# Products of the identity with itself ahead of eleven early TensorE operations

## The chip, the cores and the metric

The kernel runs on one core of a Trainium2 chip. The core has a matrix engine (TensorE, in the profile PE for its matmuls and PEld for its weight loads), a vector engine (VectorE, DVE), a scalar engine (ScalarE, ACT), GpSimd (POOL) and the engine whose queue issues the transfers (SyncE, SP). Each takes its own instructions in the order in which they stand; they wait for each other on semaphores. The metric is the device time of one execution in microseconds, as the median of the runs.

## The reference

Two attentions follow each other (32 packed queries `p` attend to `k` and `v`; then `q` attends to the packed result), and the output goes through two feed-forward blocks:

```python
p_packed = sm_attn(p, k, v)                 # batch 8, heads 8, seq 576, head_dim 64
out = sm_attn(q, p_packed, p_packed)
x = out.transpose(0, 2, 1, 3).reshape(B * S, H * D)          # 4608 x 512
h = x @ w_in                                # d_ff 1024
solu = h * softmax(h)
ln = (solu - mu) / np.sqrt(var + 1e-06) * g_ln
y = ln @ w_out
r = np.maximum(y @ w2_in, 0.0)              # d_ff 2048
return (r * r) @ w2_out
```

The weights arrive as 64-bit floats and are turned into 32-bit ones on the chip.

## The kernel before

All work is first put into a list: `plan.op` and `plan.either` note an operation with its engine, a function that issues its instructions, and the buffers that it reads and writes. There are 5182 such operations, numbered as they are noted. `Plan.emit` (lines 372 to 396) then goes through the table `ORDER` (line 22), written out by hand, and issues the operations in that order. Since each engine takes its instructions in order, `ORDER` is each engine's queue.

For each of the 8 batches, `pack` (the first attention) issues on TensorE: the scores `s1` of `p` and `k` (`scores`, matmul in line 661), three groups of three transposes `pt` of the exponentials (line 725), the products `ppp` with `v` (line 736), and three transposes `ptp` (lines 752 and 753). `unpack` (the second attention) issues the scores `s2` of `q` (line 661 again) and the products `pg` of the packed result with `w_in` (line 672, `tiles8`), which become the tile `G`. `h_tile` issues the products `ph` of the attention weights with `G` (line 832 for the first batch, in plain 32-bit floats; line 855 for later ones and for the tile that spans two batches) and the transposes `ptv` of the normalised result (line 899). `y_stage` multiplies by `w_out` (lines 555 to 557). The second feed-forward block follows from about 463 us.

Between those TensorE operations VectorE and ScalarE do the softmax (maxima `mx`, line 691; exponentials `e`, line 708; copies `eT` of the transposes, line 537; scalings `pp` and `pd`, lines 740 and 742; transposes `a` of the second scores, line 770; sums `d`, line 795) and, in the same queues, the decoding of the weights (lines 570 to 601).

The results of all these products except `ph` lie in four PSUM banks that are shared. A bank is bound to a buffer when the first operation that names the buffer is issued, and goes back to the end of a list of free banks after the last one that does:

```python
    def bank(name):
        return psm.tile([P, 512], F32, name, tag="m", bufs=4, shared=True)
...
                    if b in uses and b.slot is None:
                        b.slot = free.setdefault(b.ring, list(range(b.ring.bufs))).pop(0)
```

`s1` and `s2` take all four banks at once; the `ph` tiles have two places of two banks each in another pool. The first matmul into a buffer waits until the engines that read the bank's buffer before have done so. A plain 32-bit product issues two weight loads and two matmuls on the chip, a transpose one of each: the 72 products of `ppp` in the code are 144 matmuls in the profile, the 9 transposes of `pt` are 9.

## Time and profile before

| | us |
|---|---|
| median of 3 runs | 1197.12 |
| lowest and highest | 1196.34, 1198.63 |
| the profiled execution | 1201.08 |
| its span, from the first to the last instruction | 1199.3 |

| engine | busy us | share of the span |
|---|---|---|
| TensorE matmuls | 1153.4 | 96% |
| TensorE weight loads | 1079.8 | 90% |
| VectorE | 918.8 | 77% |
| ScalarE | 757.5 | 63% |
| GpSimd | 128.9 | 11% |

The shares are means over the whole span, and the change is about its first 80 us. [...] The clock is listed as a mean over a stretch, from events that are recorded from 42.9 us on.

### The profile page before, as it was taken

The numbers are of one execution on the slowest core, as the hardware profiler recorded it, in microseconds if no ns is written. First come the engines' busy times: TensorE is split into PE (matmuls) and PEld (weight loads), VectorE is DVE, ScalarE is ACT, GpSimd is POOL, SyncE is SP. The second block draws the span as 40 slices with busy tenths as digits, with TensorE's granted clock in tenths as the row PEclk, the third lists the DMA queues.
The fourth block names the chain that finished last, engine by engine and source line by source line (L and its number), as shares of the span: only waits on it lengthen the run. The fifth ranks groups of instructions, "written<-read, shape, count | busy, mean of one in ns | idle before, by whom it ended". The sixth has DMA issues, their size and how long they took to land.

```text
span 1199.3 us, 26114 instructions
## 1 busy us (share of the span) xinstructions
PE 1153.4 (96%) x10044; PEld 1079.8 (90%) x10044; DVE 918.8 (77%) x1849; ACT 757.5 (63%) x1600; POOL 128.9 (11%) x137
## 2 busy tenths in 40 slices
PE   2689999999999999999999999999999999999998
PEld 1347988878898999999999999999999999999998
DVE  6999897898868853778878676734888888888885
ACT  7687766767677673576745667876545454545452
POOL 1344233023222310000000000000000000000000
PEclk9899999999999999999999999999999999999999
DMA  9633564445225499878674648557983626262602
GB/s 332 232 110 111 165 188 155 149 134 154 64 88 161 141 283 329 286 222 255 212 235 165 231 157 261 175 184 255 406 304 92 191 74 189 76 190 75 192 19 54
DMA packets 171080, 218.80 MB, mean 182 GB/s; under 512 B 17353, under 2 KB 133577, under 8 KB 170185
## 3 DMA queue, kind: packets, MB, share of 16 engines
q1 hardware_dynamic: 170089, 216.32, 55.5%
q8 instruction: 79, 1.29, 0.4%
q10 hardware_dynamic: 864, 0.79, 0.3%
q14 instruction: 48, 0.39, 0.1%
HBM read 131.08 MB, written 85.98 MB: 181 GB/s over the span
## 4 chain that ended last, share of the span: by engine, by line
PE 87%; DVE 5%; DMA 3%; ACT 3%; issue 1%; SPq 1%; POOL 0%; DVEq 0%; ACTq 0%
PE px L555 10%; PE px L557 10%; PE px L556 10%; PE ph L855 8%; PE py L555 5%; PE py L557 5%; PE py L556 5%; PE pa L555 5%; PE pa L557 5%; PE pa L556 5%; PE pz L555 3%; PE ptv L899 2%; PE pz L556 2%; PE pz L557 2%; PE s L661 2%; PE pg L672 1%
## 5 line engine op out<-in xcount | busy, mean ns | idle before, releaser
L537 ACT CAST cb<-ga 128x384 fp32r<-128x384 f32 x336 | 168.0, 514 | 163.2 <-PE pa L557 70.1
L540 DVE TENSOR_TENSOR cb<-ga,cb 128x384 fp32r<-128x384 f32 x336 | 180.4, 553 | 59.2 <-ACT cb L537 57.8
L555 PE MATMUL py<-v,wo 128*128 128x256 f32 x576 | 167.0, 290 | 0.9 <-ACT ysb L922 0.6
L557 PE MATMUL py<-v,wo 128*128 128x256 f32 x576 | 162.8, 283 | 0.0
L556 PE MATMUL py<-v,wo 128*128 128x256 f32 x576 | 162.7, 282 | 0.0
L557 PE MATMUL px<-oi,cb 128*128 128x256 f32 x504 | 142.2, 282 | 0.8 <-DVE cb L540 0.8
L555 PE MATMUL px<-oi,cb 128*128 128x256 f32 x504 | 142.2, 282 | 0.6 <-ACT gw L1135 0.6
L556 PE MATMUL px<-oi,cb 128*128 128x256 f32 x504 | 142.0, 282 | 0.0
L555 PE MATMUL pa<-oi,cb 128*128 128x256 f32 x504 | 142.0, 282 | 0.0
L557 PE MATMUL pa<-oi,cb 128*128 128x256 f32 x504 | 142.0, 282 | 0.0
L556 PE MATMUL pa<-oi,cb 128*128 128x256 f32 x504 | 142.0, 282 | 0.0
L555 PE MATMUL px<-y,zi 128*128 128x384 f32 x384 | 130.1, 339 | 1.7 <-ACT gw L1104 1.5
L557 PE MATMUL px<-y,zi 128*128 128x384 f32 x384 | 129.6, 337 | 0.0
L556 PE MATMUL px<-y,zi 128*128 128x384 f32 x384 | 129.5, 337 | 0.0
L555 PEld LDWEIGHTS py<-v,wo 128*128 128x128 f32 x576 | 110.0, 191 | 5.2 <-issue 2.1
L556 PEld LDWEIGHTS py<-v,wo 128*128 128x128 f32 x576 | 110.2, 191 | 0.9
L557 PEld LDWEIGHTS py<-v,wo 128*128 128x128 f32 x576 | 110.0, 191 | 0.0
L1048 DVE TENSOR_TENSOR ga<-ga 128x384 f32<-128x384 f32 x192 | 100.3, 551 | 5.1 <-DMA ga<-g_dram 4.2
L1104 ACT COPY gw<-px 128x384 f32<-128x384 f32 x144 | 67.2, 477 | 55.8 <-PE px L557 39.7
L1108 DVE TENSOR_TENSOR gw<-pz,gw 128x384 f32<-128x384 f32 x96 | 52.9, 553 | 62.0 <-PE pz L557 37.8
L557 PEld LDWEIGHTS px<-oi,cb 128*128 128x128 f32 x504 | 95.4, 189 | 1.1 <-DVE cb L540 1.1
L555 PEld LDWEIGHTS px<-oi,cb 128*128 128x128 f32 x504 | 95.4, 189 | 0.8 <-ACT gw L1135 0.8
(144 smaller groups left out, 2874.3 us busy)
## 6 DMA issues: line engine op xcount, KB each, us to landing
g_dram<-gw SPq DMA_DIRECT2D x192, 192.0 KB
ga<-g_dram SPq DMA_DIRECT2D x96, 384.0 KB
zi<-z_dram SPq DMA_DIRECT2D x28, 512.0 KB
oi<-o_dram SPq DMA_DIRECT2D x24, 512.0 KB
kr<-in_k_dram SPq DMA_DIRECT2D x16, 576.0 KB
vr<-in_v_dram SPq DMA_DIRECT2D x16, 576.0 KB
qr<-in_q_dram SPq DMA_DIRECT2D x16, 576.0 KB
y_dram<-ysb SPq DMA_DIRECT2D x72, 128.0 KB
```

The lines of the kernel that those rows point to most:

```text
L537: plan.op(ACT, c_act(cols, sbuf=r[0].pool not in (psm, psh, pso)), at, lambda: nc.scalar.copy(out_(), in_()), r=r, w=w)
L540: plan.either(on(cols, *engines), at, lambda e: vec[e].tensor_tensor(out_(), in_(), hi_().bitcast(F32), op=ALU.subtract), r=r, w=w, port=i ...
L555: nc.tensor.matmul(ps, lh, rh, start=first, stop=False, skip_group_check=onto)
L556: nc.tensor.matmul(ps, lh, rl, start=False, stop=False, skip_group_check=onto)
L557: nc.tensor.matmul(ps, ll, rh, start=False, stop=last, skip_group_check=onto)
L661: nc.tensor.matmul(banks[g][u]()[32 * e:32 * e + 32, :SH].rearrange("p (m t) -> p m t", t=T), lhs(ps, e, f), ts[e // 2]()[ps, e % 2, :, f] ...
L672: nc.tensor.matmul(banks[g]()[32 * e:32 * e + 32, :n], lhs()[ps, 32 * e:32 * e + 32], rhs(ps, g, e), start=True, stop=True)
L855: nc.tensor.matmul(ph()[:, fs], al[l]()[:, g], g_tiles[b, g]()[:, r, fs], start=ends[0] and g == 0 and t == 0, stop=ends[1] and g == NG - ...
L899: nc.tensor.transpose(pt()[:, c * P:(c + 1) * P], e()[:, (4 * t + c) * P:(4 * t + c + 1) * P], ident)
L1048: plan.op(DVE, c_dve(cols), at, lambda: nc.vector.tensor_tensor(out_(), in0(), in1(), op=op), r=r, w=w, port=True)
L1104: plan.op(ACT, c_act(HN), when(p, SN), lambda: nc.scalar.copy(t(), ps()[:, :HN]), r=[ps], w=[t])
L1108: plan.op(DVE, c_dve(HN), when(p, SN), lambda: nc.vector.tensor_tensor(t(), ps()[:, :HN], t(), op=ALU.add), r=[t, ps], w=[t])
```

## The change

Ahead of eleven TensorE operations, `emit` now issues a number of products of the 128 x 128 identity `ident` (plain 32-bit) with itself. They are written into the first 128 columns of the first PSUM buffer of the operation that follows, which begins that buffer anew with its own first product. Nothing reads what they leave.

```diff
+WARM = {9: 44, 30: 20, 36: 9, 41: 9, 77: 1, 82: 1, 161: 4, 196: 15, 182: 1, 207: 2, 375: 3}
...
-    def emit(self):
+    def emit(self, warm):
...
+                if i in WARM:
+                    warm(next(b for b in o.bufs if b.pool and b.pool.kw.get("space") == PSUM), WARM[i])
                 o.fn(list(o.engines)[i in second])
...
     second()
-    plan.emit()
+
+    def warm(b, n):
+        for _ in range(n):
+            nc.tensor.matmul(b()[:, :P], ident, ident, start=True, stop=True, skip_group_check=True)
+
+    plan.emit(warm)
```

The keys are numbers of operations. In the order of TensorE's queue, with the place in the profile of before:

| operation | what it is | starts at us | products ahead of it |
|---|---|---|---|
| 9 | `s1`, batch 0 | 15.62 | 44 |
| 30 | first three of the nine `pt`, batch 0 | 23.33 | 20 |
| 36 | `ppp`, batch 0 | 27.93 | 9 |
| 41 | `ptp`, batch 0 | 32.71 | 9 |
| 77 | `s2`, batch 0 | 34.07 | 1 |
| 82 | first half of `pg`, batch 0 | 38.61 | 1 |
| 161 | `s1`, batch 1 | 43.87 | 4 |
| 196 | first half of the first `ph` tile | 49.45 | 15 |
| 182 | first `pt`, batch 1 | 53.78 | 1 |
| 207 | first `ptv` | 68.74 | 2 |
| 375 | fifth `ph` tile | 76.70 | 3 |

That is 109 products, or 218 matmuls and 218 weight loads.

## Rows read from the trace of the kernel before

**Rows 1.** The page's busy tenths in 40 slices of the span, TensorE.
```profile
PE   2689999999999999999999999999999999999998
```

**Rows 2.** Waits of VectorE, 13 to 77 us: total, times, longest.
```profile
DVE a L770 <- PE s L661: 1.0, 1, 1.0
DVE d L795 <- ACT a L793: 0.8, 1, 0.8
```

**Rows 3.** Timeline of TensorE's matmuls: start, us, operation, count [idle before, releaser].
```profile
15.62 2.59 PE L661 MATMUL s<-kT,pT 32*32 32x288 f32 x64 [15.62 <-DVE pT L683]
23.33 2.15 PE L725 MATMUL pt<-ident,e 128*128 128x128 f32 x9 [5.13 <-ACT e L708]
27.93 2.27 PE L736 MATMUL ppp<-vr,eT 64*32 64x64 f32 x144 [2.44 <-ACT eT L537]
32.71 0.69 PE L752 MATMUL ptp<-ident,pd 128*128 128x128 f32 x2 [2.52 <-DVE pd L742]
...
34.07 1.17 PE L661 MATMUL s<-qT,ppf 32*32 32x288 f32 x2 [0.46 <-ACT ppf L537]
35.51 2.62 PE L661 MATMUL s<-qT,ppf 32*32 32x288 f32 x62 [0.27 <-issue]
38.61 3.91 PE L672 MATMUL pg<-wi,ppq 64*32 64x512 f32 x32 [0.48 <-DVE a L770]
43.87 1.59 PE L661 MATMUL s<-kT,pT 32*32 32x288 f32 x64 [1.34 <-ACT G L537]
49.45 3.78 PE L832 MATMUL ph<-G,aT 128*128 128x512 f32 x4 [3.99 <-DVE aT L802]
53.78 1.20 PE L725 MATMUL pt<-ident,e 128*128 128x128 f32 x9 [0.55 <-ACT e L708]
...
58.48 1.66 PE L736 MATMUL ppp<-vr,eT 64*32 64x64 f32 x144
...
68.74 1.06 PE L899 MATMUL ptv<-ident,e 128*128 128x128 f32 x8 [0.76 <-ACT ph L874]
69.64 3.60 PE L832 MATMUL ph<-G,aT 128*128 128x512 f32 x8
...
76.70 5.40 PE L855 MATMUL ph<-G,ah 128*128 128x512 f32 x8 [0.97 <-ACT ph L874]
...
102.17 2.30 PE L672 MATMUL pg<-wi,ppq 64*32 64x512 f32 x32
```

**Rows 4.** The page's costliest groups, weight loads of the `py` products: busy, mean ns | idle before.
```profile
L555 PEld LDWEIGHTS py<-v,wo 128*128 128x128 f32 x576 | 110.0, 191 | 5.2 <-issue 2.1
```

**Rows 5.** TensorE by stretches: length, busy (matmuls), mean granted clock, DMA share, GB/s.
```profile
40.00:42.00 2.00, 2.00 (x24) 1.00 0.00 0
...
46.00:48.00 2.00, 0.00 (x0) 0.58 1.02 385
...
52.00:54.00 2.00, 1.45 (x4) 0.71 1.02 354
...
76.00:78.00 2.00, 1.30 (x2) 0.76 0.94 312
```

**Rows 6.** Timeline of the other engines, 1 to 45 us.
```profile
1.15 0.29 POOL masks.py:199 TENSOR_SCALAR_AFFINE_SELECT ident<-ident 128x128 f32<-128x128 f32 x1
...
21.20 0.50 ACT L708 ACTIVATE e<-s,nmx 128x288 f32<-128x288 f32 x1 [1.62 <-DVE nmx L704]
...
26.97 1.28 ACT L537 COPY eT<-pt 128x384 f32<-128x384 f32 x3
...
31.71 0.43 DVE L740 TENSOR_SCALAR pp<-ppp,rs 128x64 f32<-128x64 f32 x2
...
35.71 1.22 DVE L586 SCALAR_TENSOR_TENSOR wraw<-wraw 128x1024 f32<-128x1024 uint32 x1
...
37.98 1.57 DVE L770 STREAM_TRANSPOSE a<-s 128x288 f32<-128x288 f32 x4 [1.05 <-PE s L661]
...
44.48 1.41 DVE L795 TENSOR_REDUCE d<-a 128x18 f32<-128x576 f32 x2 [0.76 <-ACT a L793]
```

## The prediction

> **What bounds the kernel now.** The page's slices come first [rows 1]: from the fourth slice on TensorE is busy nine tenths or more, and each slice is 30 us. The end is therefore the moment at which TensorE begins to be fed without a break, plus a sum of matmuls that the change leaves as it is. Only what moves the first 80 us moves the end.

> Which engine sets the pace in those 80 us is read from VectorE's waits [rows 2]. In 64 us it waits for TensorE's stage twice, 1.05 us ahead of `a` and 0.76 us ahead of `d` [rows 6]. Apart from those two places its queue goes on whatever TensorE does, so an earlier TensorE can give the early stretch at most 1.05 + 0.76 = 1.81 us. TensorE's own timeline [rows 3] then shows gaps of 0.3 to 5.1 us and the same operation at two paces: `s1` 2.59 us at 15.62 and 1.59 us at 43.87, `pt` 2.15 and 1.20, `pg` 3.91 and 2.30, four `ph` matmuls 3.78 us where eight take 3.60.

> The clock by stretches [rows 5] explains the later slow places. A mean of 0.58 over 46 to 48 us is full speed for 0.32 us and half for the rest: the clock fell at 46.3, 0.9 us after `s1` ended (43.87 + 1.59). By the same working it rose at 53.2, 3.7 us after the `ph` stretch began at 49.45, and fell at 77.0, 0.3 us after the gap of 0.97 us ahead of 76.70.

> For 40 to 42 us the recorded clock is 1.00 [rows 5], yet `pg` runs there in 3.91 us against 2.30 later [rows 3]. I go by the durations: everything up to 42 us runs at the lower of the two levels. By the recorded clock there would be no slow stretch ahead of 42.9 us, and the sum would be that of the fourth rival below. [...]

> **What one product costs.** It is two matmuls of 128 columns, an operation that the trace does not have with these operands. The nearest is a `ph` matmul of 512 columns in plain 32-bit: 3.60 us for eight [rows 3], 0.45 us each, a quarter of it for 128 columns, twice that for a product: 0.225 us at full clock and 0.45 us at half. The transposes `pt`, also 128 columns, give 1.20/9 x 2 = 0.27 with the last one's tail in it. From above: if a weight load (0.191 us [rows 4]) did not overlap the next, a product would cost 0.38 us. I take 0.225, since `pt` has as many loads as matmuls and shows no such pace.

> **Operation 9, 44 products.** `ident` is ready at 1.44 us [rows 6] and the bank is unused. If the clock rises 3.7 us after the first of them, as at 53.2, then 8.2 products pass at 0.45 us and 35.8 at 0.225: 3.7 + 8.1 us, ending at 13.3. `s1` starts at 15.62 as before, when VectorE's `pT` is there. Cost nothing; the cover is TensorE's empty time ahead of 15.62. A faster `s1` brings nothing either: the first `e` starts 3.0 us after the slow `s1` ends (21.20 against 18.21), so VectorE's queue lies between.

> **Operation 30, 20 products: the place that decides.** `s1` holds all four shared banks, and `pt` gets the one that comes free first, that of the first `e` [rows 6], read until 21.70. The products can't start before. The gap of 5.13 us ahead of `pt` [rows 3] is thus only 1.6 us long for them. TensorE has been idle since `s1` (17.2 to 18.2), four times the 0.9 us after which the clock fell at 46.3, so I take it as low again. With a rise 3.7 us after 21.75, 8.2 products go at 0.45 and 11.8 at 0.225: 3.7 + 2.65, ending at 28.1. `pt` starts 4.8 us late and, now at the full pace of 1.20, ends at 29.3 instead of 25.48. Behind it on TensorE stand `ppp` and all the rest; on ScalarE the copies `eT` move from 26.97 to about 28.6 and end at 29.9.

> Bounds. Were the clock still high, 20 x 0.225 = 4.5 us, ending at 26.25. Were it low throughout, 20 x 0.45 = 9.0, ending at 30.75.

> **Operations 36 and 41, 9 products each.** Their banks were read before (by the last `e` and by an `eT`), so they follow the operation ahead at once. After `pt`: 29.3 + 2.0 = 31.3, later than `eT` (29.9), so `ppp` starts at 31.3 and ends at 31.3 + 1.66 = 33.0 instead of 30.2. VectorE took it up at 31.71 [rows 6], so `pp` is **1.3 us late**. After `ppp`: 33.0 + 2.0 = 35.0, where `pd` is ready at 34.0 (`pp` + 1.0, as 32.71 is to 31.71), so `ptp` starts at 35.0. `s2` follows by no more than the 1.36 us of before (34.07 - 32.71): 36.4, and takes 1.6 at full clock, to 38.0, where before it ended at 38.13.

> **What VectorE makes of it.** Its queue carries the 1.3 us as far as the decoding step that ended at 36.93 [rows 6], now 38.2. `s2` is done by then, so the wait of 1.05 ahead of `a` is gone and `a` starts at 38.2, 0.25 late. `pg` waits for the first part of `a`, passes one product (0.225) and takes 2.30 instead of 3.91: it ends 1.1 us earlier, so ScalarE is no longer late for `d` and the 0.76 goes too. Sum at `d`: 1.3 - 1.05 - 0.76 = **-0.5 us**. The products of 77 and 82 are in this. Those of 161 (0.9 us in a gap of 1.34) hide behind VectorE, which has `d` to do until 45.9; without that cover they cost up to 0.9.

> **Operations 196 and 182.** The `ph` place is new, so 15 x 0.225 = 3.4 us fit into 3.99. If the clock has fallen, they last up to 6.8 less what a rise gives back, and `ph` then runs at 1.98 or so instead of 3.78; `pt` at 53.78 waits for `e` anyway. Nothing either way.

> **Operations 207 and 375.** Here the gap is itself the wait for the bank: `ptv` uses one that `a` of `s2` reads, `ph` one that the square of an earlier tile reads [rows 3]. The products stand behind that wait and add their whole length. The 0.45 us of 207 is made good, since the next `s1` waits for VectorE in the middle of its matmuls. The 3 of 375 are 0.7 us on the path from which TensorE is the bound. They come after the gap, so they can't keep the clock from falling at 77.0.

> **Sum:** +1.3 - 1.05 - 0.76 + 0.68 = **+0.2 us**. The profiled execution, 1201.08 us, would take 1201.3; its span is 1.8 us shorter than that, and it lies 4.0 us above the median of the runs shown. The difference is carried to the median: 1197.12 + 0.2 = **1197.3 us**.

> **Rivals.**
> 1. *Both clocks are kindlier: faster.* The clock is still high at 21.75 and does not fall at 77. Then `pt` starts at 26.25, ends at 27.45, `ppp` starts at 29.5 and ends at 31.15, ahead of 31.71: no delay at `pp`, and 0 - 1.81 + 0.68 = -1.1 us. The eight `ph` at 76.70 take 3.60 instead of 5.40: -1.8. Together -2.9, **1194.2**. For it: whether the clock falls depends on what stands just before, and that is moved. Against: 3.5 us or more of idle time ahead of 21.75. Chance 0.27.
> 2. *Only the second happens:* 0.2 - 1.8 = -1.6, **1195.5**. Chance 0.10, and no measurable change.
> 3. *A product costs 0.38: slower.* By 0.38 (0.76 at half clock) the first 44 last until about 20.0, `s1` ends at 21.6 instead of 18.2, and the bank of `pt` is free up to 3.4 late, at 25.1. Then 20 x 0.38 = 7.6, `pt` to 33.9, 9 x 0.38 = 3.4, `ppp` to 39.0: `pp` 7.3 late. With -1.81 and +1.1: **1203.7**. It decides from 0.28 us a product, where the 44 no longer fit ahead of 15.62. For it: the loads' 191 ns; against: `pt`. Chance 0.16.
> 4. *The recorded clock is right up to 42.9:* only the products run at 0.225, all else as recorded. `pt` 26.25 to 28.4, `ppp` 30.4 to 32.7, `ptp` at 34.7, `s2` at 36.1 for 4.06 us, ending 2.0 late, and VectorE with it: 2.0 + 0.7 = +2.7, **1199.8**. Chance 0.05.

> **How the numbers follow.** The forecast has 0.42. Its own range comes from the bounds of operation 30: full clock gives -1.1 (1196.0); low throughout makes `pp` 2.65 us later still, +2.9 (1200.0). A measurement of this kernel can tell about 0.2%, 2.4 us. Faster by more than that is rival 1: 0.27. Within: the forecast and rival 2, 0.52. Slower: rivals 3 and 4, 0.21. The range reaches from rival 1 to the forecast's upper end, 1194.2 to 1200.0, and leaves out rival 3.

> **What would show it.** In the profile of the changed kernel: the first 44 products done by about 13 us; the 20 of operation 30 starting at 21.7 to 21.8, not at 17 to 18, and `pt` at about 28; VectorE's `pp` at 33; no wait ahead of `a` and `d`; `s2` in 1.6 us and `pg` in 2.3; three products after the square, ahead of the fifth `ph` tile. The prediction is wrong if the 20 start as soon as `s1` ends, if the clock is high when they start, if a product takes far more than 0.23 us, or if what is won or lost by 80 us does not reach the end because a later wait of TensorE takes it up.

## The result, and the profile of the changed kernel

| | before | after |
|---|---|---|
| median of 6 runs each, us | 1198.20 | 1204.46 |
| lowest and highest | 1196.34, 1199.80 | 1203.11, 1205.42 |
| the profiled execution, its span | 1201.08, 1199.3 | 1203.39, 1201.6 |

The ratio of after to before is 1.0052 [1.0041, 1.0062]: slower by half a per cent, 6 us, where 1197.3 was forecast and the range ended at 1200.0. Line numbers of after stand 5 higher than those of before from `emit` on; the products are line 1303.

The page of after, its busy tenths of TensorE in 40 slices and the row of its instruction queue (packets, MB, share):

```profile
PE   7899999999999999999999999999999999999998
...
q8 instruction: 80, 1.31, 0.5%
```

The first two slices are fuller than in [rows 1], 7 and 8 for 2 and 6, and the end came later: the products are themselves counted as busy. TensorE's timeline of after, columns as in [rows 3]:

```profile
1.49 12.67 PE L1303 MATMUL s<-ident 128*128 128x128 f32 x88 [1.49 <-POOL ident masks.py:199]
15.29 1.60 PE L666 MATMUL s<-kT,pT 32*32 32x288 f32 x64 [1.12 <-DVE pT L688]
21.51 7.54 PE L1303 MATMUL pt<-ident 128*128 128x128 f32 x40 [4.62 <-ACT e L713]
28.88 1.15 PE L730 MATMUL pt<-ident,e 128*128 128x128 f32 x9
29.86 2.17 PE L1303 MATMUL ppp<-ident 128*128 128x128 f32 x18
31.96 1.52 PE L741 MATMUL ppp<-vr,eT 64*32 64x64 f32 x132
33.98 0.33 PE L741 MATMUL ppp<-vr,eT 64*32 64x64 f32 x12 [0.50 <-issue]
...
37.31 1.64 PE L666 MATMUL s<-qT,ppf 32*32 32x288 f32 x64 [0.24 <-ACT ppf L542]
...
40.38 1.95 PE L677 MATMUL pg<-wi,ppq 64*32 64x512 f32 x32
...
45.22 1.60 PE L666 MATMUL s<-kT,pT 32*32 32x288 f32 x64 [1.80 <-DVE pT L688]
46.75 3.62 PE L1303 MATMUL ph<-ident 128*128 128x128 f32 x30
50.21 1.88 PE L837 MATMUL ph<-G,aT 128*128 128x512 f32 x4
52.90 0.49 PE L1303 MATMUL pt<-ident 128*128 128x128 f32 x2 [0.81 <-ACT e L713]
54.35 1.87 PE L730 MATMUL pt<-ident,e 128*128 128x128 f32 x9 [0.96 <-ACT e L713]
56.02 4.66 PE L837 MATMUL ph<-G,aT 128*128 128x512 f32 x8
60.60 1.66 PE L741 MATMUL ppp<-vr,eT 64*32 64x64 f32 x144
...
78.72 0.94 PE L1303 MATMUL ph<-ident 128*128 128x128 f32 x6 [0.97 <-ACT ph L879]
79.49 3.60 PE L860 MATMUL ph<-G,ah 128*128 128x512 f32 x8
...
86.76 0.39 PE L560 MATMUL py<-v,wo 128*128 128x256 f32 x1
...
232.80 1.48 PE L741 MATMUL ppp<-vr,eT 64*32 64x64 f32 x129
236.43 0.34 PE L741 MATMUL ppp<-vr,eT 64*32 64x64 f32 x15 [2.15 <-issue]
...
265.23 1.66 PE L741 MATMUL ppp<-vr,eT 64*32 64x64 f32 x144
```

VectorE's longest waits of after in 13 to 80 us, columns as in [rows 2]. The two of before are gone; two others have come:

```profile
DVE pp L745 <- PE ppp L741: 3.0, 1, 3.0
DVE nm L867 <- PE ph L837: 1.6, 1, 1.6
```

TensorE by stretches: length; busy time and instructions of TensorE's matmuls, its weight loads, VectorE, ScalarE and GpSimd; then granted clock, DMA share and GB/s. The clock fell at 20.6 us, rose at 27.4, and fell again at 54.7 (0.50 over 22 to 24 us, 1.00 over 28 to 30, the two values that before's record also has; so 0.68 over 54 to 56 us is 0.7 us at 1.00 and 1.3 at 0.50):

```profile
20.00:22.00 2.00, 0.49 (x2) 0.49 (x3) 2.00 (x6) 1.14 (x5) 0.00 (x0) 0.65 1.05 383
...
26.00:28.00 2.00, 2.00 (x14) 2.00 (x14) 1.67 (x3) 0.70 (x1) 0.00 (x0) 0.65 0.92 296
...
54.00:56.00 2.00, 1.65 (x9) 1.65 (x10) 2.00 (x6) 1.70 (x7) 0.00 (x0) 0.68 0.99 301
```

The kernel before was profiled a second time (`again`, no edit; 1199.71 us, span 1197.9; the median of before on that chip is 1198.06). Its timeline of TensorE:

```profile
27.93 2.27 PE L736 MATMUL ppp<-vr,eT 64*32 64x64 f32 x144 [2.41 <-ACT eT L537]
...
34.08 2.69 PE L661 MATMUL s<-qT,ppf 32*32 32x288 f32 x64 [0.46 <-ACT ppf L537]
...
42.73 1.59 PE L661 MATMUL s<-kT,pT 32*32 32x288 f32 x64 [1.35 <-ACT G L537]
48.31 3.54 PE L832 MATMUL ph<-G,aT 128*128 128x512 f32 x4 [3.99 <-DVE aT L802]
52.64 1.20 PE L725 MATMUL pt<-ident,e 128*128 128x128 f32 x9 [0.79 <-ACT e L708]
...
57.34 1.66 PE L736 MATMUL ppp<-vr,eT 64*32 64x64 f32 x144
...
75.58 3.70 PE L855 MATMUL ph<-G,ah 128*128 128x512 f32 x8 [0.97 <-ACT ph L874]
...
81.39 1.48 PE L736 MATMUL ppp<-vr,eT 64*32 64x64 f32 x129
84.28 0.34 PE L736 MATMUL ppp<-vr,eT 64*32 64x64 f32 x15 [1.41 <-issue]
84.56 0.39 PE L555 MATMUL py<-v,wo 128*128 128x256 f32 x1
...
230.55 1.66 PE L736 MATMUL ppp<-vr,eT 64*32 64x64 f32 x144
...
260.68 1.52 PE L736 MATMUL ppp<-vr,eT 64*32 64x64 f32 x132
263.14 0.33 PE L736 MATMUL ppp<-vr,eT 64*32 64x64 f32 x12 [0.94 <-issue]
```

and, of VectorE's waits in 13 to 80 us, the longest; none ahead of `a` is listed:

```profile
DVE d L795 <- ACT a L793: 0.8, 1, 0.8
```

This is the better yardstick, being nearer the median, though it is one execution too. The stretch of 0.27 us inside `s2` and the fall of the clock at 77 us [rows 3, 5] are in the execution that the prediction read and not in this one; here `s2` is whole, the fifth `ph` tile takes 3.70 us, and VectorE waits 0.8 us ahead of `d` but not ahead of `a`. Where after stands against it, by the starts of the same operations:

| operation | again | after | late by |
|---|---|---|---|
| `ppp`, batch 0 | 27.93 | 31.96 | 4.0 |
| `s2`, batch 0 | 34.08 | 37.31 | 3.2 |
| `s1`, batch 1 | 42.73 | 45.22 | 2.5 |
| `pt`, batch 1 | 52.64 | 54.35 | 1.7 |
| `ppp`, batch 1 | 57.34 | 60.60 | 3.3 |
| fifth `ph` tile | 75.58 | 79.49 | 3.9 |
| first `py` behind the third `ppp` | 84.56 | 86.76 | 2.2 |
| sixth `ppp` | 230.55 | 232.80 | 2.3 |
| seventh `ppp` | 260.68 | 265.23 | 4.6 |
| end of the span | 1197.9 | 1201.6 | 3.7 |

Two things move the numbers. Up to 80 us the change loses 3.9 us, in its own steps and a stretch of 0.50 us. From there to 266 us the lateness jumps only where one of the kernels has an empty stretch put down to "issue", which means that no wait explains it, inside a `ppp`: 1.41 and 0.94 us in again, 2.15 us in after, whose 0.50 us lies in the first 80. Later it drifts between 1.9 and 4.4 us and ends at 3.7. Part of that drift belongs to the execution and not to the kernel: at 466.5 us again's TensorE waits 1.4 us for ScalarE's `ysb`, in the first profile of before 0.6 us; there `change_again`, a second profile of the change, waits 1.4 us and after less than 0.2.

### The profile page after: what moved, and what is told of

It reads as the page before. It is cut to its first block, busy times and chain, and to the rows that moved or that the text cites. A ratio compares the mean times of both kernels' runs of the same rounds, so it can differ in the third digit from the quotient of the medians.

```text
span 1201.6 us, 26545 instructions
## 1 busy us (share of the span) xinstructions
PE 1174.7 (98%) x10262; PEld 1106.9 (92%) x10262; DVE 918.5 (76%) x1849; ACT 757.7 (63%) x1600; POOL 128.9 (11%) x137
## 3 DMA queue, kind: packets, MB, share of 16 engines
q8 instruction: 80, 1.31, 0.5%
## 4 chain that ended last, share of the span: by engine, by line
PE 84%; DVE 6%; DMA 4%; ACT 3%; issue 1%; SPq 1%; POOL 0%; DVEq 0%; ACTq 0%
PE px L560 9%; PE px L562 9%; PE px L561 9%; PE ph L860 8%; PE py L560 5%; PE py L562 5%; PE py L561 5%; PE pa L560 5%; PE pa L562 5%; PE pa L561 5%; PE ptv L904 2%; PE pz L560 2%; PE pz L562 2%; PE pz L561 2%; DMA g_dram<-gw 2%; PE s L666 1%
```

## The experiments

Each kernel is the change with another table `WARM`; only products come, go or move to operation 9, where TensorE has nothing else to do until 15.6 us. Ratios are to the kernel before on the same chip. Theory A is the bank of operation 30: its 20 products can't start before 21.5 us and stand in series with the 9 of operation 36 ahead of `ppp`. The other theory (B, later B2) is that added instructions move the places in TensorE's instruction stream at which it stalls. What a letter means in an expectation, the expectation says.

**One part alone, or left out.**

```diff
 again: no edit (the kernel before)
```

> The kernel before once more, unchanged, for a second execution with a profile. Theory A (the early stretch decides; the profiled execution of before was a slow one): about 1197 to 1199 us, that is 2 to 4 us below the first profile's 1201.08, with the clock's fall at 77 us or TensorE's empty stretch of 1.40 us at 85.66 gone. Theory B (executions differ by places after 100 us, in TensorE's waits for instructions or data): the first 100 us look as in the first profile, and the difference lies later.

Measured: 1199.71 us, one run, and the rows above. The fall of the clock at 77 us is gone, as theory A had it; the stretch of 1.4 us in the third `ppp` is not, and the time lies above A's 1197 to 1199.

```diff
+WARM = {9: 44, 36: 9, 41: 9, 77: 1, 82: 1, 161: 4, 196: 15, 182: 1, 207: 2, 375: 3}   # no30
```

> All products but the 20 of operation 30. Theory A (the 20, held back by the bank, then the 9 of operation 36 behind them, make VectorE wait 3.0 us at pp): pt starts at 23.3 again, VectorE's wait at pp is under 0.5 us, and most of the loss is gone: 1197 to 1200 us. Theory B (the 436 added instructions of TensorE shift the places where its queue runs empty, wherever they stand): 356 of 436 are still there, so 1203 us or more.

Measured: 1198.55 us, 1.0008 [0.9996, 1.0020]. Without the 20, the loss is gone within what can be told. But it also moved every later instruction by 80 places, and of the stretches inside a `ppp` one of 1.09 us is left, in the fifth. Another of 1.31 us stands among the `ph` of line 860, at 147 us, where before has none.

```diff
+WARM = {30: 20}   # only30
```

> Only the 20 products of operation 30. Theory A: pt starts at about 29 as with all products, but ppp follows pt at once, so pp is no more than 1 us late; with the two waits of VectorE (1.05 and 0.76 us) gone the early stretch is level with before or up to 1 us ahead: 1196.5 to 1199.5 us, which says that the loss needs 30 and 36 in series. If the 20 alone cost what the whole change costs, 1203 to 1205. Theory B: 80 of 436 instructions, so a fifth of the loss, about 1199.5.

Measured: 1197.18 us, 0.9996 [0.9986, 1.0007]. The suspect alone costs nothing that shows; before's two stretches have gone as well, for one of 1.08 us in the fifth `ppp`. Its timeline of TensorE:

```profile
21.89 6.98 PE L1303 MATMUL pt<-ident 128*128 128x128 f32 x40 [3.71 <-ACT e L713]
30.48 1.66 PE L741 MATMUL ppp<-vr,eT 64*32 64x64 f32 x144 [0.62 <-ACT eT L542]
```

The bank holds the products back to 21.89 us as A says. Without the 9 of operation 36, though, `ppp` starts at 30.48 and VectorE waits 0.5 us at `pp`, not 3.0.

```diff
+WARM = {9: 44}   # only9
```

> Only the 44 products of operation 9. Theory A: they end ahead of s1, the early stretch is that of before, and the time is that of before within 1 us: 1197 to 1199. Theory B: 176 of 436 instructions, two fifths of the loss: about 1200.5, with TensorE's empty stretches (1.40 us at 85.66, 0.87 us at 264.98 in before) at other places or of another length.

Measured: 1201.15 us, 1.0023 [1.0012, 1.0035]. Products that stand in an empty stretch and delay no operation (`s1` starts at 15.68 us) make the kernel slower. The profiled execution took 1198.90 us and is one of the shorter of the twelve, so it can't show all that the median holds. The chain that ended last in only9 (start, us, what):

```profile
229.63 1.41 PE ppp L741 x91
231.04 2.42 issue
233.46 0.47 PE ppp L741 x16
```

and its TensorE by stretches, columns as in those of after:

```profile
232.00:234.00 2.00, 0.54 (x17) 0.37 (x17) 0.00 (x0) 0.00 (x0) 1.48 (x3) 0.80 0.03 5
234.00:236.00 2.00, 2.00 (x10) 2.00 (x11) 1.36 (x5) 0.59 (x1) 0.00 (x0) 0.50 0.43 130
```

In the middle of the sixth `ppp`, the profile has no instruction of TensorE for 2.42 us while nothing is waited for, and the clock then falls at 233.2. Before has no gap there. The view of the transfers of only9 over 231 to 232 us has one packet on TensorE's instruction queue (packets, MB, share of 16 engines):

```profile
q8 instruction: 1, 0.02, 6.0%
```

It runs from 231.09 to 232.05 us and carries 16,384 bytes, as does each of the 79 packets of that queue in before and of the 80 in after; TensorE goes on 1.41 us after its end. So TensorE was waiting for its instructions, as I read it; the counts that follow test that. I counted TensorE's instructions (a weight load and a matmul for each matmul record, plus the semaphore instructions recorded on TensorE). A `ppp` is 288 of them in 1.5 us. In again the stretches come at numbers 1728 and 6336, in only9 at 5567, in the change at 704 and 5824: each is, to one, 192 more than a multiple of 256. From the rows: again's third `ppp` starts at number 1470, and 129 matmuls later it is 1728. Such numbers are 256 apart, one packet by the count: 20,170 instructions in 79 packets in before, 255 each, and 20,601 in 80 in after, 258 each. Inside a `ppp`, a stall appears where it begins at or just ahead of such a number and so takes in two of them. An estimate from these rows says why two are needed: from the start of the packet to the next matmul are 2.37 us in only9 (231.09 to 233.46), in which `ppp`, at 288 instructions in 1.5 us, would use up some 450. A product is 4 instructions (109 products are 218 matmuls and 218 weight loads more in the page of after), so 64 products move everything by exactly 256, and by this count where the stalls of a `ppp` fall depends on the total modulo 64. The tables that follow test that. The rule for a `ppp` doesn't cover the shorter stretches outside `ppp`, but they obey the same count: no30's 1.31 us stands at number 3520, 192 beyond a multiple of 256, and the 0.27 us in `s2` of before at 447.

**Totals of 64 and 128 (before's places), and 109 without operation 36.**

```diff
+WARM = {9: 64}   # only9_64
```

> 64 products ahead of operation 9 and none elsewhere. The empty stretches of TensorE that no engine explains lie, in every profile so far, inside ppp and at places of its instruction stream that differ by multiples of about 255 instructions. A product is 4 instructions, so 64 of them are about one such step and the stretches should stand in the same operations as in before. Theory B2 (what counts is where those steps fall, not how many products there are): the 1.4 us stretch in the third ppp and the 0.9 us one in the sixth come back at the same matmuls as in before, and the time is that of before, 1198 to 1199.5 us, less than the 1201.15 with 44 products. Theory B1 (each added instruction costs): more than with 44, 1202 to 1203.

Measured: 1199.43 us, 1.0008 [0.9996, 1.0020]: twenty products more than only9 and not slower than before. The stretches are back at before's two places, in the third and the seventh `ppp` (the expectation calls it the sixth), at 1984 and 6592 (1728 and 6336 plus 256), and `s2` has one of 0.58 us at 703 (447 plus 256).

```diff
+WARM = {9: 63, 30: 20, 36: 9, 41: 9, 77: 1, 82: 1, 161: 4, 196: 15, 182: 1, 207: 2, 375: 3}   # all_128
```

> The whole change with 63 instead of 44 products at operation 9, 128 in all, so that everything behind operation 375 lies two steps later than in before. The 63 end at about 17 us, ahead of the moment at which VectorE takes up s1 at 19.4. Theory A with B2 (the bank costs 3 to 4 us in the early stretch, the rest of the loss is where the steps fall): about 1202 us, 2 to 3 less than the change. Theory A alone: as the change, 1204.5. Theory B1: 1205 or more.

Measured: 1201.10 us, 1.0027 [1.0016, 1.0038]; stretches at 2239 and 6847. VectorE's wait at `pp` is 1.0 us, and `nm` is not waited for: the clock rose at 25.2 us here, so that the 20 products took 6.25 us and not 7.54.

```diff
+WARM = {9: 19, 36: 9, 41: 9, 77: 1, 82: 1, 161: 4, 196: 15, 182: 1, 207: 2, 375: 3}   # no30_64
```

> The change without the 20 of operation 30 and with 19 instead of 44 at operation 9, 64 products in all. Theory A with B2: the early stretch is within 0.5 us of that of before and the steps fall as in before: 1197.5 to 1199 us. Theory B1: 64 products' worth of loss, 1201.5 or more.

Measured: 1199.26 us, 1.0012 [0.9999, 1.0025]; stretches at 1984 and 6592.

```diff
+WARM = {9: 53, 30: 20, 41: 9, 77: 1, 82: 1, 161: 4, 196: 15, 182: 1, 207: 2, 375: 3}   # no36_109
```

> The change with the 9 products of operation 36 moved to operation 9 (53 there), 109 in all as in the change, so the steps fall as there behind operation 36. Theory A: the 20 of operation 30 alone delay pt to 29 but ppp follows it at once, VectorE's wait at pp falls from 3.0 to about 0.5 us, and the time is 2 to 2.5 us below the change: 1202 to 1202.5. If operation 30 alone makes the delay: 1204 to 1205.

Measured: 1205.41 us, 1.0053 [1.0035, 1.0071]. A's expectation fell: VectorE waits 2.2 us at `pp`, not 0.5. Timeline of TensorE:

```profile
29.68 1.52 PE L741 MATMUL ppp<-vr,eT 64*32 64x64 f32 x132 [0.62 <-ACT eT L542]
33.68 0.33 PE L741 MATMUL ppp<-vr,eT 64*32 64x64 f32 x12 [2.48 <-issue]
```

`ppp` does start 2.3 us earlier than in after, but its end is where it was (33.68 for 33.98): the stall at number 704 grew from 0.50 to 2.48 us and took the place of the 9 products. The total, and so the places, were after's.

**Totals that leave no `ppp` with two places.**

```diff
+WARM = {9: 14}   # only9_14
```

> Only 14 products ahead of operation 9, 56 instructions. In eight profiles TensorE's unexplained stretches lie inside ppp, each at a place of its instruction stream that is 192 more than a multiple of 256, and only where two such places fall into the same ppp (288 instructions long). By that count 14 products leave none of the eight ppp with two. Theory B2 (the places decide): no such stretch in the profile, where before has two of 1.4 and 0.9 us, so about 1195.5 to 1196.5 us, faster than before although nothing but idle work was added. Theory B1 (each added instruction costs): 1198.5 to 1199. Theory A says nothing here: the early stretch is that of before.

Measured: 1195.20 us, 0.9955 [0.9939, 0.9971]: faster than before. The timeline of TensorE:

```profile
15.51 2.59 PE L666 MATMUL s<-kT,pT 32*32 32x288 f32 x64 [8.79 <-DVE pT L688]
...
81.23 1.66 PE L741 MATMUL ppp<-vr,eT 64*32 64x64 f32 x144
...
260.06 1.66 PE L741 MATMUL ppp<-vr,eT 64*32 64x64 f32 x144
```

The fourteen are over 8.79 us before `s1`, which runs at the slow pace of before (2.59 us), so they warm no operation. All that they do is move the stream by 56 instructions, and the third and the seventh `ppp` are whole. One stretch of 0.59 us is left, among the `py` at 168.7 us (number 4032); with those of no30, only9_64 and before it shows that not all lie inside `ppp`, as the expectation has it. Before 450 us only9_14 gains 1.8 us on again, as much as the stretches say (2.35 less 0.59); the other 2.9 us come later, at two waits of TensorE that are shorter (0.3 for 1.4 us for ScalarE's `ysb`, 0.2 for 1.5 for VectorE's `cb`), and no run shows why.

```diff
+WARM = {9: 49, 30: 20, 36: 9, 41: 9, 77: 1, 82: 1, 161: 4, 196: 15, 182: 1, 207: 2, 375: 3}   # all_114
```

> The whole change with five more products at operation 9 (49), which end ahead of s1: 114 in all. By the same count no ppp has two of the places, neither the first one (78 products ahead of it) nor those after 100 us. Theory A with B2: what is left is the bank's cost, pp about 1 to 2.5 us late, and the 0.7 us of operation 375, less the two stretches of before: 1198 to 1200 us, some 5 less than the change. Theory A alone, or B1: 1204.5 to 1205.

Measured: 1199.28 us, 0.9991 [0.9979, 1.0004]. This is the change with five more hidden products, which end at 14.76 us, ahead of `s1`; and it is 0.4 to 0.6% better than the change (1.0052, and 1.0035 below). The early stretch has no part in that: VectorE doesn't wait at `nm`, but the clock fell at 77.5 us, the fifth `ph` tile took 4.62 us, and the first `py` behind the third `ppp` starts at 87.18 (86.76 in after). The seventh `ppp` starts at 263.38 (265.23): between them lies the sixth, without after's stretch of 2.15 us. One stretch of 0.71 us is left in the first `ppp`, at number 704, with number 448 among the products just ahead; VectorE still waits 2.5 us at `pp`.

```diff
+WARM = {9: 58, 30: 20, 41: 9, 77: 1, 82: 1, 161: 4, 196: 15, 182: 1, 207: 2, 375: 3}   # no36_114
```

> As the run with 114 products, with the 9 of operation 36 moved to operation 9 (58). The places in the stream stay where they are from operation 41 on. Theory A (20 of operation 30 and 9 of operation 36 in series make pp late): ppp follows pt at once, VectorE waits 0.5 us or less at pp, 1 to 2 us less than with 36 in place: 1196.5 to 1198. If the 20 of operation 30 make the delay alone: the same as with 36 in place.

Measured: 1198.63 us, 0.9985 [0.9973, 0.9996]; no stretch in any `ppp`, no wait at `pp`. It is not a clean partner of no36_109 (1.0053), though:

```profile
16.96 1.60 PE L666 MATMUL s<-kT,pT 32*32 32x288 f32 x64
21.94 4.73 PE L1303 MATMUL pt<-ident 128*128 128x128 f32 x40 [3.38 <-ACT e L713]
```

The 58 products hold `s1` back from 15.79 to 16.96 us, and the 20 of operation 30 then take 4.73 us for 6.08, 0.24 us each, which is the full pace. So the wait at `pp` went with the clock as well as with the stall. Against all_114 it is 0.65 us by the medians, where A had 1 to 2, and the intervals overlap: that operation 36 stands in series is seen in the timelines and not in the time.

```diff
+WARM = {9: 5, 36: 9, 41: 9, 77: 1, 82: 1, 161: 4, 196: 15, 182: 1, 207: 2, 375: 3}   # no30_50
```

> The change without the 20 of operation 30 and with 5 instead of 44 at operation 9, 50 products in all; by the count again no ppp with two places. Theory A with B2: VectorE doesn't wait at pp, its waits ahead of a and d are gone, the 0.7 us of operation 375 stay: 1195 to 1197 us. Theory B1: 50 products' worth of loss, 1200.

Measured: 1197.45 us, 0.9978 [0.9967, 0.9989], just above the range expected; no stretch.

**The change again, another clear total, and the useful parts at a clear total.**

```diff
 change_again: no edit (the change)
```

> The change itself once more, on one chip with the next two. Theory A with B2: 0.4 to 0.6% slower than before, about 7 us more than the run with 114 products showed against before; the stretch inside ppp at 236 us is there in the profile, and most of its runs list a mean clock below the 0.996 of the first profile, which had no fall behind that stretch. If its loss came from the chip that it first ran on, it would now be within 0.2% of before.

Measured: 1203.51 us, 1.0035 [1.0022, 1.0048], just under the 0.4 to 0.6% expected; its profile repeats after's, with waits of 2.9 us at `pp` and 1.6 at `nm` and the stall of 2.1 us at 236 us.

```diff
+WARM = {9: 50}   # only9_50
```

> 50 products ahead of operation 9 and none elsewhere; no ppp has two of the places 256 instructions apart. Theory B2: as 14 products, 0.3 to 0.5% faster than before, with no unexplained stretch in ppp. If the number of products counts: between 44 (0.23% slower) and 64 (0.08% slower), so not faster.

Measured: 1196.81 us, 0.9978 [0.9967, 0.9989]: six products more than only9, which had 1.0023. This is the plainest pair: in both, nothing else is added and `s1` starts at 15.7 us. No `ppp` has a stretch; 0.36 us stand in `s2` and 0.33 among the `ph`.

```diff
+WARM = {9: 11, 36: 9, 41: 9, 77: 1, 161: 4, 196: 15, 182: 1}   # best_50
```

> 50 products again, but 11 at operation 9 and the rest where the bank is free well ahead of the operation: 36, 41, 77, 161, 196, 182; none at 30, 82, 207, 375. Theory A: s2 and pg run at full clock, VectorE's wait of 0.76 us ahead of d is gone, and no product stands behind the wait that it is to fill: 0.5 to 1.5 us faster than only9_50. If higher clock in the early stretch is worth nothing: the same as only9_50.

Measured: 1195.51 us, 0.9969 [0.9958, 0.9981]; no stretch in any `ppp` (0.23 us among the `py`), no wait at `pp`, and 0.3 us ahead of `d`. `s2` ran at the full pace (1.63 us; 1.64 in after), `pg` didn't (3.70; 1.95 in after). It is 1.3 us below only9_50 by the medians, with intervals that overlap. It beats both kernels, and so does only9_14 (0.9955, on another chip); the two can't be told apart, so the products' warming is not shown to be worth anything.

Rows that differ in the total alone, or nearly, stand side by side here (operation 9's number makes up the total):

| products kept | places as in before | places clear |
|---|---|---|
| operation 9 alone | only9_64 1.0008 | only9_14 0.9955, only9_50 0.9978 |
| all but operation 30 | no30_64 1.0012 | no30_50 0.9978 |
| all | all_128 1.0027 | all_114 0.9991 |

The pairs are not quite clean: all_114 keeps one stretch of 0.71 us, and the 64 and 63 products of the left column hold `s1` back to 18.55 us in only9_64 and 17.29 in all_128. Across, clear places are worth 0.3 to 0.5%, about 4 us. The profiles show only part of that: the stretches add up to 2.4 to 3.2 us on the left and to 0 to 0.7 on the right, a difference of 2.0 to 2.6 us in each row. The rest was not traced. Down, operation 30 costs 0.13 to 0.15%, 1.8 us by the medians (1201.10 - 1199.26, 1199.28 - 1197.45); each of the two lies within the noise (each ratio has 0.12% or so either way), and operation 9 differs as well, so the size is not shown.

## Why the prediction was wrong, step by step

**What failed first: the yardstick.** "An earlier TensorE can give the early stretch at most 1.05 + 0.76 = 1.81 us." The 1.05 us ahead of `a` hang on the execution that was profiled, whose `s2` stalled: its third matmul started at 35.51, 1.44 us after the first [rows 3], and it ended at 38.13 for 36.77 in again, which has no such wait. That is a stall of the kind counted above, at number 447, and not a matter of TensorE's pace. In only9_64, where `s2` stalls at 703, the wait is back:

```profile
DVE a L775 <- PE s L666: 1.4, 1, 1.4
```

Only the 0.76 was to be had, and it was had: neither wait is in after. The sum loses 1.05 of its gains.

**Operation 30, the place that decides.** The gate was right: the 20 start at 21.51 (forecast 21.75), and the clock was low there (0.50 over 22 to 24 us). The size was not. The clock rose 5.9 us after they began, not 3.7, so they took 7.54 us, not 6.35. `ppp` started at 31.96 (31.3) and then met a stall of 0.50 us that no step had. VectorE's `pp` was 3.0 us late where the sum has 1.3. The size goes with the clock: the same 20 took 4.73 us in no36_114, at 0.24 us each as at full clock, near the 4.5 of the forecast's lower bound.

**Operations 196 and 182: "Nothing either way."** This failed. The 15 products took 3.62 us and `ph` 1.88, as worked out for full speed, so TensorE was done early and waited for `e` twice, 0.81 and 0.96 us. The clock fell at 54.7, 0.4 us after the second of those waits; `pt` took 1.87 us for 1.20, the next eight `ph` matmuls 4.66 for 3.70 in again, and VectorE waited 1.6 us at `nm`. The lateness against again grows from 1.7 us at `pt` to 3.3 at the next `ppp`. Rows of before said that the clock can fall after a gap of 0.97; the prediction saw it for 77 us and not here.

**What was right.** The 44 products end at 14.16 us (13.3), and their price at full clock is near the forecast's 0.225 (9 in 2.17 us, 0.24 each, ahead of `ppp`); `s1`, `s2` and `pg` take 1.60, 1.64 and 1.95 us. The three products behind the square cost 0.77 us (0.68), and those of operation 207 don't show at 79 us. The durations were the better witness of the clock than its record ahead of 42.9 us: `pg` takes half the time here, 1.95 us for 3.91. The three products are not shown to have kept the clock up at the fifth `ph` tile, since again has no fall at 77 us either.

With the measured sizes the sum is 3.0 - 0.76 + 1.6 + 0.77 = +4.6 us, where the starts of the fifth `ph` tile give +3.9; the remaining 0.7 was not traced.

**What was not in the sum at all: the places in the stream.** The first profile of before had three rows of it, 1.40 us of "issue" in the third `ppp`, 0.87 in the seventh and 0.27 in `s2`, and the prediction passed over them:

```profile
87.06 0.34 PE L736 MATMUL ppp<-vr,eT 64*32 64x64 f32 x15 [1.40 <-issue]
```

Visible empty time of this kind inside `ppp` is 2.35 us in again and 2.65 in after, so between just these two kernels it nearly cancels; the table shows what it hides. Against before, which has its own stretches, the change costs 0.27% with the places of before and 0.35 to 0.52% with its own 109, and with clear ones it makes no difference that can be measured. Against kernels whose places are clear too (0.9955 and 0.9978) it is still 0.13 to 0.36% slower (the smaller figure lies within the noise), so nothing says that clear places undo the early loss.

**Rival 3** gave 1203.7, close to the result by luck and not by its cause: a product does not cost 0.38 us and `pt` was not held up by the first 44.

**What stays open.** The profiles give after 3.7 us over again at the end of the span, the medians 4.6 and 6.3 us over before. The change's unprofiled runs list a mean clock of 0.992 to 0.994, the profiled one 0.996; another stretch at the low clock would do that, as the one behind the stall in only9 does, but no profile of the change shows it. Why one place inside a `ppp` stays covered in no36_114 and stands open for 0.71 us in all_114 was not settled beyond the place just ahead, nor why the eighth `ppp` shows no stretch in the four profiles in which it has two places. Part of what clear places are worth is in no profile.

## What to carry to other kernels

Adding or taking away instructions on TensorE moved every later one against the places, 256 instructions apart, at which it stalled; here that alone was worth 0.3 to 0.5%, as much as the edit (0.35 and 0.52%), so time an edit at two totals that differ by a few harmless instructions before crediting or blaming it. Work that is put into a gap can start only when its buffer is free (the 20 of operation 30 at 21.51 us, 4.6 after `s1` ended), and where it then reaches past the gap, it delays what stands behind it (`ppp` by 4.0 us against again), so give it a buffer that is free before the gap begins. Profile the kernel before twice before a wait or a clock event of one execution becomes a term of a sum.

## What the runs showed of the hardware that was not expected

Most packets cost nothing that shows: before has three such stretches for its 79 packets, after two for its 80. In a `ppp` that takes in two of the places, up to 2.48 us stood open (no36_109).

Behind one such stretch the clock fell, in only9: after the 2.42 us without a matmul the granted clock was 0.50 over 234 to 236 us, where only9_64, with twenty products more, has 1.00. Not so in no36_109: behind 2.37 us at 237 us no fall is recorded.
